# Two-attention decode kernel: the order of the first transfers, and the shape in which x is loaded

## Chip, core and metric

The kernel runs on one core of a Trainium2 chip. The metric is the device time of one execution in microseconds (us); lower is better.

## The reference

Two independent decode attentions, A and B, each for one query token. x has 576 elements; there are 32 query heads and 16 key/value heads of 128 elements, so that two query heads share a K and a V. The cache holds 8192 positions; A uses only the last 2048 of them, B uses all. Everything is bf16.

```python
W = min(4096, max(256, Sk // 4))                     # A: 2048
q = (x @ wq).reshape(B, Sq, Hq, Dh).transpose(0, 2, 1, 3)
k = jnp.repeat(k_cache[:, :, Sk - W:, :], rep, axis=1)   # B: all of k_cache
v = jnp.repeat(v_cache[:, :, Sk - W:, :], rep, axis=1)
scores = jnp.einsum("bhqd,bhkd->bhqk", q, k) * (Dh ** -0.5)
o = jnp.einsum("bhqk,bhkd->bhqd", softmax(scores), v)
return o.transpose(0, 2, 1, 3).reshape(B, Sq, Hq * Dh) @ wo
```

The output is A's row of 576 and B's row of 576, side by side. With wq and wo (576 x 4096 and 4096 x 576, 4.7 MB each) a call reads 102.76 MB.

## The kernel before

**Memory.** One SBUF tensor, `slots`, holds four areas of 4 MB: K slot 0, K slot 1 and a V area of two slots. Work goes in five groups (`NG`): group 0 is all of A, groups 1 to 4 are four key/value heads of B each. A group loads K slot 0 (4 MB), K slot 1 (4 MB) and V (8 MB). The wq tensors borrow the same areas before the first group: A's wq lies at the end of the V area, B's wq over K slot 1 and the beginning of V (`WQ`, L711). wo is loaded into areas that have come free at the end.

**Order.** Every operation is added with its engine and the resources that it reads and writes (`Program.add`). The waits are worked out from these; each engine then runs its own operations in the order in which they were added. All large transfers are issued by SP, on one queue, in this order before the change:

1. half of A's K slot 0 (`half_of_A(sp, 0, 0)`, L713): 128 rows of 16 KB. `emit` takes SP's first operation out of the list, whatever it is, and puts it ahead of the barrier at the program's start (L246 to L252);
2. A's wq, and 3. B's wq (`load`, L398): 128 rows of 36 KB each;
4. the other half of K slot 0 (`load_k(0, 0)`, L409), then K slot 1 for A as two halves (L411, L417), and V for A as four quarters (L429);
5. for B, per group, K slot 0, K slot 1 (L407) and V (L424); at the end wo in five pieces (L398).

Both halves of K slot 0 count on one semaphore (`k0`); PE begins to transpose K when it has reached 64, that is when both have landed. A's K slot 1 can be issued only when PE has read all of B's wq, which lies there.

**The query.** ACT issues two small loads of x, one for A and one for B (`load_x`, L366), each as 64 rows of nine elements into `xnine`. `twice` is a 64 x 128 selection matrix, copied by DVE from the identity (L437): one matmul (L440) multiplies `xnine` by it, so that row m of x comes out in partitions 2m and 2m + 1 of PSUM `misc`. `x_columns` (L449, four small DVE operations for each of A and B) puts the halves into the zero-padded `xpad`, with the help of the parity mask `par2`. `q_part` (L458) then makes q with 36 matmuls of 512 columns over wq, and `q_finish` turns it into columns (ACT L464, PE L469, DVE L473). On DVE the order is: `twice`, A's xpad, A's q columns, B's xpad, B's q columns, then twelve operations that build masks (L722 to L747), then copies out of the K transposes (L511).

**The stages of a group.** PE transposes K by 128 x 128 matmuls (L498), ACT and DVE copy the results (L508, L511), PE forms scores (L523), ACT takes the exponential (L549), PE transposes it (L561) and DVE masks it (L568), PE sums V (L590), DVE keeps the result (L608). In the last group the softmax weights of all groups are combined (L617 to L673) before the V sums. At the end PE multiplies by wo (L693), DVE and ACT copy out (L705) and SP stores (L707).

POOL fills constants at the start (`setup`, L375 to L377, and the selections of L383, which make the identity).

Of the kernel before, what the change touches and what calls it, by code (L numbers as in the profile page):

```python
# [4 lines left out]
BF16 = mybir.dt.bfloat16  # L5
# [9 lines left out]
SK = 8192  # L15
SCALE = DH ** -0.5
SLOT = 16384
UNIT = 4096
# [18 lines left out]
class Program:  # L37
# [15 lines left out]
    def add(self, eng, fn, reads=(), writes=(), dma=None, after=(), tag=None, inc=1, loop=None):  # L53
        op = Op(eng, fn, tuple(reads), tuple(writes), dma, tag, inc if dma is None or inc > 1 else 16, loop)
        deps = []
        for r in op.reads:
            w = self.writer.get(r)
            if w is not None:
                deps.append((w, True))
            if r[0] == "bank":  # L60
                deps += [(o, False) for o in self.readers.get(r, ())]
        for r in after:
            deps += [(o, False) for o in self.readers.get(r, ())]
        for r in op.writes:
            w = self.writer.get(r)
            if w is not None:
                deps.append((w, False))
            deps += [(o, False) for o in self.readers.get(r, ())]
        for r in op.reads:
            self.readers.setdefault(r, []).append(op)  # L70
        for r in op.writes:
            self.writer[r] = op
            self.readers[r] = []
        for o, raw in deps:
            if o is op:
                continue
            if o.dma is None and o.eng == eng and (not raw or eng in ("pe", "sp")):
                continue
            op.deps.append(o)
            o.needed = True  # L80
        op.order = len(self.ops)
        self.ops.append(op)
        return op
# [192 lines left out]
def bass_concat_heads__sliding_block_cached__gqa_block_cached__decode_kernel(  # L276
# [13 lines left out]
    xs = [A_x, B_x]  # L290
    ks = [A_k_cache, B_k_cache]
# [3 lines left out]
    W_A = min(4096, max(256, SK // 4))  # L295
# [12 lines left out]
    add = prog.add  # L308

    slots = nc.alloc_sbuf_tensor("slots", [128, 4 * SLOT], BF16)  # L310
# [3 lines left out]
    ident = nc.alloc_sbuf_tensor("ident", [128, 128], BF16)  # L314
    identf = nc.alloc_sbuf_tensor("identf", [128, 128], F32)
    pick = nc.alloc_sbuf_tensor("pick", [128, 4, 128], F32)
    pickB = nc.alloc_sbuf_tensor("pickB", [128, 4, 32], F32)
# [3 lines left out]
    selq = nc.alloc_sbuf_tensor("selq", [128, 4, 2], BF16)  # L321
    onesf = nc.alloc_sbuf_tensor("onesf", [128, 4], F32)
    qst = nc.alloc_sbuf_tensor("qst", [128, 1024], BF16)
    qcol = nc.alloc_sbuf_tensor("qcol", [128, 2, HQ], BF16)
    xnine = nc.alloc_sbuf_tensor("xnine", [64, 2, 9], BF16)
    twice = nc.alloc_sbuf_tensor("twice", [64, 128], BF16)
    xpad = nc.alloc_sbuf_tensor("xpad", [128, 2, 9, 32], BF16)
    par2 = nc.alloc_sbuf_tensor("par2", [128, 2], F32)
    maskV = nc.alloc_sbuf_tensor("maskV", [128, 4], F32)
# [11 lines left out]
    warm = nc.alloc_sbuf_tensor("warm", [128, 8], F32)  # L341
# [5 lines left out]
    misc = nc.alloc_psum_tensor("misc", [128, 512], F32)  # L347
# [4 lines left out]
    B_M = ("bank", 7)  # L352
# [4 lines left out]
    KS = [[("k", 0)], [("k", 1, 0), ("k", 1, 1)]]  # L357
    VS = [("v", 0), ("v", 1), ("v", 2)]
    koff = lambda s: s * SLOT
# [3 lines left out]
    def load_x(P):  # L363
        def go(act):
            with nc.allow_non_contiguous_dma(reason="small x load"):
                return act.dma_start(xnine[:, P, :], xs[P][0, 0, :].rearrange("(m r) -> m r", m=64))  # L366
        add("act", go, writes=[("xnine", P)], dma="x%d" % P)

    load_x(0)
# [1 line left out]


    def setup(pool):
        for t in (ident, xpad, selq, warm, identf, pick, pickB, qst):
            pool.memset(t[:], 0.0)  # L375
        pool.memset(onesf[:], 1.0)
        return pool.memset(opj[:], 0.0)  # L377

    add("pool", setup, writes=["ident", ("xpad", 0), ("xpad", 1), "selq", "ones", "warm", "identf", "pick", "pickB",
                               ("qst", 0), ("qst", 1), ("opj", 0), ("opj", 1)])  # L380

    def select(t, base_, pattern, mult):
# [18 lines left out]
    def load_k(g, s):  # L401
        dst = slots[:, koff(s):koff(s) + SLOT]

        def go(sp):
            if g:
                i = 4 * (g - 1) + s
                return sp.dma_start(dst, ks[1][0, i:i + 3:2, :, :].rearrange("e (p t) d -> p e (t d)", t=128))  # L407
            if s == 0:
                return half_of_A(sp, s, 1)  # L409
            op.also.append((32, half_of_A(sp, s, 0)))  # L410
            return half_of_A(sp, s, 1)  # L411
        op = add("sp", go, writes=KS[s], dma="k%d" % s, inc=64 if g or s else 32)

    def half_of_A(sp, s, m1):
        i = 8 * m1 + s
        src = ks[0][0, i:i + 7:2, SK - W_A:, :].rearrange("h (p t) d -> p h (t d)", t=64)
        return sp.dma_start(slots[:, koff(s) + m1 * 2 * UNIT:koff(s) + (m1 + 1) * 2 * UNIT], src)  # L417

    def load_v(g):
        dst = slots[:, VOFF:VOFF + 2 * SLOT]  # L420

        def go(sp):
            if g:
                return sp.dma_start(dst, vs[1][0, 4 * g - 4:4 * g, :, :].rearrange("h (p t) d -> p h (t d)", t=256))  # L424
            for i in range(4):
# [4 lines left out]
                if i < 3:  # L430
# [3 lines left out]

    add("dve", lambda dve: dve.tensor_copy(twice[:, :].rearrange("p (m e) -> p m e", e=2),  # L437
                                           bass.AP(tensor=ident, offset=0, ap=[[128, 64], [1, 64], [0, 2]])),
        reads=["ident"], writes=["twice"])
    add("pe", lambda pe: pe.matmul(misc[:, 320:338], lhsT=twice[:, :], rhs=xnine[:, :, :].rearrange("p a r -> p (a r)"),  # L440
                                   start=True, stop=True),
        reads=[("xnine", 0), ("xnine", 1), "twice"], writes=[B_M])

# [263 lines left out]
            reads=[("outsb", P, k) for k in range(P + 1)], writes=[("out", P)], dma="out%d" % P)  # L709

    WQ = [(4 * SLOT - WQ_W, [("v", 2)]), (SLOT, [("k", 1, 0), ("k", 1, 1), ("v", 0)])]  # L711

    add("sp", lambda sp: half_of_A(sp, 0, 0), writes=["first"], dma="k0", inc=32)  # L713
    for P in range(2):
        off, res = WQ[P]
        x_columns(P)
# [9 lines left out]
        reads=["kindA"], writes=["sameA"])  # L726
# [3 lines left out]
        reads=["sameB0"], writes=["sameB"])  # L730
# [3 lines left out]
    def pick_A(dve):  # L734
# [8 lines left out]
        reads=["sameB0", "pickB"], writes=["pickB"])  # L743
# [3 lines left out]
        reads=["four"], writes=["maskP"])  # L747
    for g in range(NG):
        for s in range(2):
            load_k(g, s)  # L750
        load_v(g)
        for s in range(2):
            q_stage(g, s)
        k_transpose(g, 0, 0)
        k_transpose(g, 1, 1)
        for u in range(2, 8):
            k_scores(g, u - 2, 2 * u)
            k_transpose(g, u, 2 * u + 1)
        k_scores(g, 6, 16)
        k_scores(g, 7, 17)  # L760
        softmax_exp(g)
        for c in range(2):
            softmax_transpose(g, c, 18 + c / 2)
        if g == NG - 1:
            weights_top(g)
            weights_exp(g)
            weights_sum(g)
            combine(range(NG - 1), (g, 19.3, LAST))
            o_columns(0)
        v_sums(g)  # L770
        v_keep(g)
# [47 lines left out]
```

## Time and profile before

| | us |
|---|---|
| three runs | 246.78, 246.80, 247.11; median 246.8 |
| the profiled execution, its own time | 246.78 |
| its span, first to last instruction | 245.3 |
| outside the span | 1.5 |
| A's x: issue to landing | 8.8 |
| B's x: issue to landing | 15.3 |
| A's wq: issue to landing | 17.2 |
| B's wq: issue to landing | 27.7 |
| spread of x (L440) starts | 17.32 |
| A's query (L458) starts | 18.67 |
| B's query (L458) starts | 29.55 |
| SP issues A's K slot 1 | 33.30 |
| first K transpose (L498) starts | 34.53 |

All times in views are microseconds from the start of the span. A line of a timeline has the start, the duration, the engine, the line of the kernel, the operation and its output and inputs; in brackets the engine's idle time before it and what ended it. SPq is SP's sequencer, PEld the weight load of TensorE. The trace has a record of each packet that a DMA engine moved as well, with start, duration and size; where a number comes from these and not from a view, the text says "packet records".

### The profile page before, as it was taken

The page shows a single profiled execution, that of the slowest core. Times are in us where ns is not written, and L with a number is a line of the kernel's source. Part 1 is how long each engine was busy: PE and PEld are TensorE (multiplying, and loading weights), DVE is VectorE, ACT ScalarE, POOL GpSimd, SP SyncE. Part 2 cuts the span into 40 slices and gives each one's busy share as a digit, 9 for nine tenths or more (in the row PEclk, how much of TensorE's full clock was granted, in tenths as well). Part 3 has the DMA queues.
Part 4 walks back from the last instruction along what each step waited for, and adds up shares of the span by engine and source line. Part 5 has one row for each costly group of instructions (what it writes and reads, how often), then busy time and mean ns, then how long its engine had stood idle before and what let it go on. Part 6 is the DMA issues. An engine that isn't in the chain of part 4 may idle for free. (4 is left out here: it accounts for less than half of the span.)

```text
span 245.3 us, 5212 instructions
## 1 busy us (share of the span) xinstructions
PE 161.8 (66%) x2325; PEld 115.8 (47%) x2325; DVE 87.8 (36%) x152; ACT 92.7 (38%) x96; POOL 6.3 (3%) x33
## 2 busy tenths in 40 slices
PE   0006188695368997184999454999647599845964
PEld 0002056563226684133878221978432687635753
DVE  0011039475206545202555312265522256533030
ACT  2000037575104776200778400577620378630000
POOL 5000000000000000000000000000000000000000
PEclk9999689998559999757899757599968799977699
DMA  7999989999999999999999999999999999999994
GB/s 313 444 451 397 423 345 417 430 427 430 446 425 427 450 470 417 395 438 433 492 402 481 406 395 427 427 460 460 395 406 427 438 470 438 438 397 439 416 406 176
DMA packets 4064, 102.88 MB, mean 419 GB/s; under 512 B 596, under 2 KB 728, under 8 KB 984
## 3 DMA queue, kind: packets, MB, share of 16 engines
q1 hardware_dynamic: 3896, 102.76, 97.7%
q8 instruction: 6, 0.10, 0.2%
q10 hardware_dynamic: 160, 0.00, 0.0%
q14 instruction: 2, 0.02, 0.0%
HBM read 102.76 MB, written 0.00 MB: 419 GB/s over the span
## 5 line engine op out<-in xcount | busy, mean ns | idle before, releaser
L508 ACT ACTIVATE kt<-ktps 128x1024 bf16<-128x1024 bf16 x80 | 79.3, 1039 | 84.1 <-PE ktps L498 84.0
L498 PE MATMUL ktps<-ident,slots 128*128 128x128 bf16 x1280 | 83.5, 227 | 16.3 <-PEq L214 15.7
L498 PEld LDWEIGHTS ktps<-ident,slots 128*128 128x128 bf16 x1280 | 77.3, 102 | 32.1 <-issue 32.0
L511 DVE COPY kt<-ktps 128x1024 bf16<-128x1024 bf16 x80 | 60.4, 772 | 48.9 <-PE ktps L498 48.9
L590 PE MATMUL opsum<-slots,ptm 128*32 128x512 bf16 x320 | 28.8, 536 | 14.3 <-PEq L214 14.3
L590 PEld LDWEIGHTS opsum<-slots,ptm 128*32 128x32 bf16 x320 | 14.0, 129 | 27.6 <-issue 25.6
L523 PE MATMUL sacc<-kt,qst 128*32 128x512 bf16 x320 | 25.4, 392 | 2.3 <-PEq L214 2.3
L608 DVE TENSOR_TENSOR vtmp<-opsum,maskV 128x512 f32<-128x512 f32 x4 | 2.8, 692 | 34.8 <-PE opsum L590 34.8
L561 PE MATMUL misc<-ident,psb 128*128 128x128 bf16 x40 | 4.6, 288 | 15.8 <-PEq L214 15.8
L549 ACT ACTIVATE psb<-sacc,stat 128x2048 bf16<-128x2048 f32 x5 | 9.8, 1967 | 9.7 <-DVE stat L538 9.7
L561 PEld LDWEIGHTS misc<-ident,psb 128*128 128x128 bf16 x40 | 3.5, 129 | 18.2 <-issue 18.2
L440 PE MATMUL misc<-xnine,twice 64*128 64x18 bf16 x1 | 0.2, 173 | 17.3 <-DMA xnine<-in_B_x_dram 17.3
L568 DVE TENSOR_TENSOR ptm<-misc,maskP 128x1024 bf16<-128x1024 bf16 x5 | 3.5, 692 | 16.0 <-PE misc L561 16.0
L523 PEld LDWEIGHTS sacc<-kt,qst 128*32 128x32 bf16 x320 | 5.0, 94 | 8.3 <-issue 4.7
L705 ACT ACTIVATE outsb<-ktps 64x144 bf16<-64x144 f32 x1 | 0.3, 287 | 21.5 <-PE ktps L693 21.5
L693 PE MATMUL ktps<-slots,opj 128*32 128x144 bf16 (+1 forms) x192 | 6.8, 247 | 2.3 <-DMA slots<-in_B_wo_dram 2.3
L440 PEld LDWEIGHTS misc<-xnine,twice 64*128 64x128 bf16 x1 | 0.1, 102 | 17.3 <-issue 17.3
L458 PE MATMUL turned<-slots,xpad 128*32 128x512 bf16 x36 | 3.7, 590 | 5.9 <-DMA slots<-in_B_wq_dram 5.9
L464 ACT ACTIVATE qrow<-opsum 128x512 bf16<-128x512 f32 x1 | 0.6, 597 | 18.4 <-PE opsum L458 18.4
L693 PEld LDWEIGHTS ktps<-slots,opj 128*32 128x32 bf16 x192 | 5.2, 97 | 3.8 <-DMA slots<-in_B_wo_dram 3.0
L473 DVE CAST qcol<-misc 128x32 bf16<-128x32 f32 x2 | 0.6, 300 | 15.4 <-PE misc L469 15.4
L449 DVE TENSOR_SCALAR xpad<-misc,par 128x5 bf16<-128x5 f32 (+1 forms) x8 | 1.2, 229 | 12.4 <-PE misc L440 12.4
(76 smaller groups left out, 58.2 us busy)
## 6 DMA issues: line engine op xcount, KB each, us to landing
slots<-in_B_k_cache_dram SPq DMA_DIRECT2D x8, 4096.0 KB
slots<-in_A_k_cache_dram SPq DMA_DIRECT2D x4, 2048.0 KB
slots<-in_A_v_cache_dram SPq DMA_DIRECT2D x4, 2048.0 KB
slots<-in_A_wq_dram SPq DMA_DIRECT2D x1, 4608.0 KB, 17.2
slots<-in_B_wq_dram SPq DMA_DIRECT2D x1, 4608.0 KB, 27.7
slots<-in_A_wo_dram SPq DMA_DIRECT2D x1, 4608.0 KB, 19.7
slots<-in_B_wo_dram SPq DMA_DIRECT2D x1, 3024.0 KB, 26.5
slots<-in_B_wo_dram SPq DMA_DIRECT2D x1, 1008.0 KB, 9.3
```

The lines of the kernel that those rows point to most:

```text
L449: add("dve", lambda dve, dst=dst, o=320 + 9 * P + i, n=n, e=e: dve.tensor_scalar(dst, misc[:, o:o + n], par2[:, e:e + 1], None, ALU.mult), ...
L458: ins = pe.matmul((turned if P else opsum)[32 * j:32 * j + 32, :], lhsT=xpad[:, P, u, :], rhs=slots[:, o:o + 512], start=(u == 0), stop=(u ...
L498: ins = pe.matmul(ktps_bf[q][:, t * 128:(t + 1) * 128], lhsT=slots[:, o:o + 128], rhs=ident[:, :], start=True, stop=True, is_transpose=True)
L508: add("act", lambda act, src=src, dst=dst: act.activation(dst, src, ACT.Copy), reads=[("bank", q)], writes=[("kt", u % NKT, q)], tag="e%d% ...
L511: add("dve", lambda dve, src=src, dst=dst: dve.tensor_copy(dst, src), reads=[("bank", q)], writes=[("kt", u % NKT, q)], tag="e%d%d" % (u, q))
L523: ins = pe.matmul(sacc[32 * j:32 * j + 32, :], lhsT=qst[:, o:o + 32], rhs=rhs, start=(u == 0 and e == 0), stop=True, skip_group_check=True)
L549: return act.activation(dst, src, ACT.Exp, bias=st(C_NB + g), scale=SCALE, accum_out=st(C_L + g))
L561: ins = pe.matmul(dst[:, t * 128:(t + 1) * 128], lhsT=psb[:, o:o + 128], rhs=ident[:, :], start=True, stop=True, is_transpose=True)
L568: return dve.tensor_tensor(ptm[:, c * 1024:(c + 1) * 1024].rearrange("p (t y) -> p t y", t=8), dst.rearrange("p (t y) -> p t y", t=8), mas ...
L590: ins = pe.matmul(opsum[64 * j + 32 * x:64 * j + 32 * x + 32, :], lhsT=ptm[:, o:o + 32], rhs=v[:, at[0], at[1], :, :, b:b + 128], start=(n ...
L608: add("dve", lambda dve: dve.tensor_tensor(vtmp[:, :, :], src, by, ALU.mult), reads=[B_O, w], writes=["vtmp"], tag="keep")
L693: ins = pe.matmul(ktps[P + j // 2][32 * j:32 * j + 32, 0:w], lhsT=opj[:, P, at:at + 32], rhs=slots[:, o:o + w], start=(jj == 0), stop=(jj ...
```

## The change

x comes as 16 rows of 36 elements for A and for B. `twice` becomes four selection matrices of 16 x 128, one for each quarter of such a row; POOL clears it (it is no longer written as a whole) and one DVE copy sets its ones. Four matmuls, one for each quarter, accumulate into the same place of PSUM as the single one did. The half of K slot 0 is no longer loaded ahead of everything: SP's first operation, which is issued ahead of the barrier, is now A's wq, and both halves of K slot 0 follow B's wq. Everything else is as it was.

```diff
-    xnine = nc.alloc_sbuf_tensor("xnine", [64, 2, 9], BF16)
-    twice = nc.alloc_sbuf_tensor("twice", [64, 128], BF16)
+    xnine = nc.alloc_sbuf_tensor("xnine", [16, 2, 36], BF16)
+    twice = nc.alloc_sbuf_tensor("twice", [16, 4, 128], BF16)
...
-                return act.dma_start(xnine[:, P, :], xs[P][0, 0, :].rearrange("(m r) -> m r", m=64))
+                return act.dma_start(xnine[:, P, :], xs[P][0, 0, :].rearrange("(m r) -> m r", m=16))
...
-        for t in (ident, xpad, selq, warm, identf, pick, pickB, qst):
+        for t in (ident, twice, xpad, selq, warm, identf, pick, pickB, qst):
             pool.memset(t[:], 0.0)
...
-            if s == 0:
-                return half_of_A(sp, s, 1)
-            op.also.append((32, half_of_A(sp, s, 0)))
-            return half_of_A(sp, s, 1)
-        op = add("sp", go, writes=KS[s], dma="k%d" % s, inc=64 if g or s else 32)
-
-    def half_of_A(sp, s, m1):
-        i = 8 * m1 + s
-        src = ks[0][0, i:i + 7:2, SK - W_A:, :].rearrange("h (p t) d -> p h (t d)", t=64)
-        return sp.dma_start(slots[:, koff(s) + m1 * 2 * UNIT:koff(s) + (m1 + 1) * 2 * UNIT], src)
+            for m1 in range(2):
+                i = 8 * m1 + s
+                src = ks[0][0, i:i + 7:2, SK - W_A:, :].rearrange("h (p t) d -> p h (t d)", t=64)
+                ins = sp.dma_start(dst[:, m1 * 2 * UNIT:(m1 + 1) * 2 * UNIT], src)
+                if m1 == 0:
+                    op.also.append((32, ins))
+            return ins
+        op = add("sp", go, writes=KS[s], dma="k%d" % s, inc=64)
...
-    add("dve", lambda dve: dve.tensor_copy(twice[:, :].rearrange("p (m e) -> p m e", e=2),
-                                           bass.AP(tensor=ident, offset=0, ap=[[128, 64], [1, 64], [0, 2]])),
-        reads=["ident"], writes=["twice"])
-    add("pe", lambda pe: pe.matmul(misc[:, 320:338], lhsT=twice[:, :], rhs=xnine[:, :, :].rearrange("p a r -> p (a r)"),
-                                   start=True, stop=True),
-        reads=[("xnine", 0), ("xnine", 1), "twice"], writes=[B_M])
+    add("dve", lambda dve: dve.tensor_copy(bass.AP(tensor=twice, offset=0, ap=[[512, 16], [130, 4], [8, 16], [1, 2]]),
+                                           bass.AP(tensor=ident, offset=0, ap=[[128, 16], [0, 4], [1, 16], [0, 2]])),
+        reads=["ident", "twice0"], writes=["twice"])
+
+    def x_spread(pe):
+        for c in range(4):
+            ins = pe.matmul(misc[:, 320:338], lhsT=twice[:, c, :], rhs=xnine[:, :, 9 * c:9 * c + 9],
+                            start=(c == 0), stop=(c == 3))
+        return ins
+    add("pe", x_spread, reads=[("xnine", 0), ("xnine", 1), "twice"], writes=[B_M])
...
-    add("sp", lambda sp: half_of_A(sp, 0, 0), writes=["first"], dma="k0", inc=32)
```

More of the change, by code (lines that the diff above doesn't have):

```diff
@@ L377, in setup @@
         return pool.memset(opj[:], 0.0)
-    add("pool", setup, writes=["ident", ("xpad", 0), ("xpad", 1), "selq", "ones", "warm", "identf", "pick", "pickB",
+    add("pool", setup, writes=["ident", "twice0", ("xpad", 0), ("xpad", 1), "selq", "ones", "warm", "identf", "pick", "pickB",
                                ("qst", 0), ("qst", 1), ("opj", 0), ("opj", 1)])
```

## Prediction

> **What bounds the kernel now.** I read the page from the top: engines, slices, queues.
>
> ```profile
> PE 161.8 (66%) x2325; PEld 115.8 (47%) x2325; DVE 87.8 (36%) x152; ACT 92.7 (38%) x96; POOL 6.3 (3%) x33
> ...
> DMA  7999989999999999999999999999999999999994
> ...
> q1 hardware_dynamic: 3896, 102.76, 97.7%
> ```
>
> No compute engine is over two thirds busy. The transfers that SP issues (q1) fill 97.7% of 16 engines' span, 239.7 of 245.3 us. So the kernel is one stream of 102.76 MB, and only a stretch in which the DMA engines stand still can be won. There is one slice below 9 in the middle, the sixth from the left (slice 5, 0-based), besides the first and the last. The table of windows of 1 us shows that place (columns: stretch and its length, busy us of each engine, clock, DMA share, GB/s):
>
> ```profile
> 32.00:33.00 1.00, 1.00 (x16) 0.32 (x8) 0.00 (x0) 0.00 (x0) 0.00 (x0) 0.61 0.99 426
> 33.00:34.00 1.00, 0.29 (x10) 0.04 (x2) 0.00 (x0) 0.60 (x1) 0.00 (x0) 1.00 0.39 164
> 34.00:35.00 1.00, 0.68 (x13) 0.62 (x14) 0.71 (x4) 0.00 (x0) 0.00 (x0) 1.00 0.65 197
> 35.00:36.00 1.00, 1.00 (x22) 1.00 (x20) 0.97 (x7) 0.82 (x1) 0.00 (x0) 1.00 0.77 328
> ```
>
> The stream falls from 426 to 164 GB/s and is back after 36. SP's own waits and the timeline there name the cause:
>
> ```profile
> SPq L417 <- PE turned L458: 30.3, 1, 30.3
> ```
>
> ```profile
> 32.51 0.74 PE L458 MATMUL turned<-slots,xpad 128*32 128x512 bf16 x8
> 33.30 1.20 SPq L417 DMA_DIRECT2D slots<-in_A_k_cache_dram  x2
> ```
>
> SP waits until the last B-query matmul has read B's wq, since A's second K slot lies over it; it issues that K load at 33.30. The packet records show the last packets of the transfer ahead (the second half of A's first K slot) ending engine by engine from 33.38 to 34.03, and the first packets of the new load starting from 34.64 to 35.10: 1.34 us from issue to first packet. Summed over the 16 engines, the idle time between 33.0 and 35.5 is **1.11 us** of the stream. Nowhere else between 6 and 240 us do the records show one.
>
> The chain of waits shows that this counts at the end:
>
> ```profile
> 227.62 5.08 PE opsum L590 x57
> ...
> 232.72 0.33 SPq L398
> ...
> 233.09 10.06 DMA slots<-in_B_wo_dram
> 243.15 0.04 issue
> ```
>
> The last wo loads are issued at 232.72, but the wo transfer ahead of them keeps the engines until 237.26 and later. With 1.34 us to the first packet they come 3.2 us early, and the stream, not PE, sets 243.15. What is taken out of the stream comes off the end.
>
> [...] once started, one x packet goes with each wq packet (7.0, 8.4, 9.8 us, steps of 1.37), but the first x packet goes at 5.58, 4.2 us after its issue at 1.39, when an engine has passed about seven 16 KB packets. [...]
>
> **The change part by part.**
>
> 1. *Order of the stream.* Before: half of K slot 0, A's wq, B's wq, the other half. After: A's wq, B's wq, both halves. The bytes ahead of K slot 1 are the same, so K slot 0 still ends at 33.4 to 34.0. What moves is wq. The records price the half slot at 8 packets of 0.611 us per engine, 4.9 us, and a wq at 8 of 1.364 us, 10.9 us. So A's wq lands about 12.6 to 13.4 (18.6 before) and B's at 23.6 to 24.3 (29.2 before). The B query starts on landing and takes, as now, 3.75 us from its first matmul (29.55) to SP's issue (33.30). K slot 1 is issued near **28.3**, when over 5 us of K slot 0 are still to be moved. The 1.34 us to the first packet are hidden, and the gap goes.
>    Worth: 1.11 us of idle engines. The restart too: 12 of the 16 first packets after the gap took 0.87 instead of 0.611 us, 12/16 x 0.26 = 0.19. Sum **1.30 us**. The start keeps its slow first packets; with 36 KB packets they may cost nothing to 0.2 us more. I take off 0.1.
> 2. *The hoisted issue.* SP's instruction ahead of the barrier is now wq's (0.38 us) in place of half a K slot (0.69). First packet at 1.41 us in either case. Behind the barrier SP issues B's wq and two halves, 0.53 + 2 x 0.6, done near 3.2. Cost nothing; the cover is the 10.9 us of the first wq.
> 3. *x.* Eight x rows per engine become two, with two semaphore writes as before: 4 x packets per engine in place of 10. Each costs the stream about 0.012 us, so 0.07 us are won. Arrival: not before 1.39 + 1.34 = 2.7 plus four turns; at the latest, if seven packets of 36 KB pass first, 1.66 + 7 x 1.364 = 11.2, then three more turns of 1.37, 15.3. I take 15. The spread may then be later than A's wq, but 2 us earlier than the 17.3 of now.
> 4. *Four matmuls.* Three more at up to 0.17 us (the one of now takes 0.173), at most 0.5 us. On the path x to spread to xpad to A query to xpad B to B query: 0.8 us for spread and xpad, 5.7 from the first A-query matmul to B's xpad ready (18.67 to 24.41), 0.5 for the new matmuls. From x at 15.3: 22.3, before B's wq at 23.6. Hidden by wq's landing. If that cover went, it would cost at most 0.5.
> 5. *POOL and DVE.* One memset of 512 elements more: near 0.53 us (pick, 128x512). It holds up ident, behind which par2 and twice wait on DVE (at 4.6 now, then 5.2). The copy into twice has 128 elements a row as before, 0.26. All under x, which comes no earlier than about 7. Nothing.
> 6. *Later.* K slot 1 lands 1.3 us earlier, and so does every transfer behind it. Who could be late next is an issue whose release does not move: V at 75.3 with the queue full to 83.5, V at 112.0 with 122.3, wo at 212.7 with 219.2, the last wo at 232.7 with 237.3. The smallest margin is the last, 4.5 less 1.34. The first K transposes follow a pause of PE of 5 us where there was almost none, [...] DVE's twelve mask operations (34.4 to 36.7, ahead of the first K copies now) move to about 30. PE now stands idle from 44.7 to 47.0 waiting for K slot 1, so this has room.
>
> Sum against the profiled execution's own time: 246.78 - 1.30 + 0.1 - 0.07 = 245.5; since a restart elsewhere or the landing of the slowest engine may eat a little, I take **1.2 us: 245.6**. That execution lies at the lower end of the three runs, 0.02 under their median of 246.8.
>
> **The rivals.**
>
> *x comes too late (slower).* x now stands behind 36 KB packets from the start. From the spread to SP's K issue the path takes 0.8 + 0.5 + 5.7 + 3.75 = 10.8 us. The issue must be made by about 32.0 (33.4 - 1.34), so the spread by 21.2; at 22.5 the gap is as large as now, and beyond that each us costs one. If the first x packet had to wait for both wq transfers (16 packets, 23.5 us) and the other turns fall among K packets, the spread comes at 25.4, the K issue at 36.2, the first packet at 37.5: a gap of 3.8 + 0.2 in place of 1.3, **249.5**. For it: the 4.2 us that x waits now are not explained by turns. Against: the wait now is seven packets, not sixteen, and the four turns after it end at 15.3.
>
> *The gain is given back (same).* Earlier landings meet a PE that is not earlier, because its clock falls in other places, and the last wo issue comes late. This needs PE's last V sums to be over 3.2 us later against the stream[...]. Time **246.7**. V sums of the first stage already start 3.7 us after V has landed (69.6 against 65.9), for a reason the views do not give.
>
> *Half the gain.* The engines finish K slot 0 more unevenly, or the start on 36 KB packets is slower: 0.6 us, **246.2**.
>
> *The change does not do what it says:* wq would not be first on the wire. The hoist takes whatever SP operation stands first, and with the half slot gone that is wq; I give it nothing.
>
> **How the numbers follow.** Gap closed, 245.6 (245.3 to 245.9): 0.78. Half the gain, 246.2: 0.08. Given back: 0.08. x too late: 0.06. What a measurement can tell from no change is about 0.2%, 0.5 us. Faster by more: 0.78 + 0.08 = 0.86; same 0.08; slower 0.06. The range of 245.2 to 246.3 takes in the first two cases.
>
> **What would show it.** SP's wait for the B query ends near 28.3 instead of 33.3; the windows from 33 to 36 stay above 380 GB/s; A's query starts between 13 and 17; PE resumes on K slot 1 near 45.7 instead of 46.97; the last landing is at 241.9 instead of 243.15. A gap elsewhere, a spread after 21 us, or a wo issue that comes after its queue has run dry would prove me wrong.

## The result, and the profile after

The changed kernel takes **245.37 us** (median of 6 runs, 245.18 to 245.63), the kernel before 246.99 (6 runs): a ratio of 0.9937 with a 95% interval of 0.9924 to 0.9950, or 1.6 us less. A second measurement, 245.46 beside 247.35, gave 0.9925 (0.9912 to 0.9938). The profiled execution took 245.18 us, its span is 243.8 us; before these were 246.78 and 245.3.

The page of the changed kernel, slices and queues:

```profile
DMA  9999999999999999899999999999989999989994
...
q1 hardware_dynamic: 3896, 102.76, 98.3%
q10 hardware_dynamic: 64, 0.00, 0.0%
```

The 8 in the sixth slice has become a 9, and the same bytes fill more of a shorter span. The x queue has 64 packets in place of 160. SP's waits and its timeline around the change (start, duration, instruction):

```profile
SPq L411 <- PE turned L460: 26.3, 1, 26.3
```

```profile
28.86 1.20 SPq L411 DMA_DIRECT2D slots<-in_A_k_cache_dram  x2
30.10 1.25 SPq L427 DMA_DIRECT2D slots<-in_A_v_cache_dram  x2
```

SP still waits for B's query before K slot 1, but the wait ends at 28.86 instead of 33.30, and the windows of 1 us show what this does to the stream (the last columns are clock, DMA share and GB/s; a packet counts whole in the window in which it starts, so a share can pass 1):

```profile
32.00:33.00 1.00, 0.00 (x0) 0.00 (x0) 0.22 (x1) 0.00 (x0) 0.00 (x0) 0.89 1.07 459
33.00:34.00 1.00, 0.00 (x0) 0.00 (x0) 0.00 (x0) 0.00 (x0) 0.00 (x0) 0.50 1.08 459
34.00:35.00 1.00, 0.33 (x4) 0.36 (x5) 0.00 (x0) 0.00 (x0) 0.00 (x0) 0.50 0.88 377
35.00:36.00 1.00, 1.00 (x12) 1.00 (x10) 0.00 (x0) 0.28 (x1) 0.00 (x0) 0.50 1.11 475
```

Before, the last three had 164, 197 and 328 GB/s. The chain of waits ends as before, with wo:

```profile
227.83 4.97 PE opsum L592 x59
...
232.82 0.33 SPq L398
...
233.19 8.42 DMA slots<-in_B_wo_dram
241.61 0.04 issue
```

PE's last V sums end at the same time as before (232.80 against 232.70). The last wo landing, which waits for the stream, comes 1.54 us earlier (241.61 against 243.15). That is the gain of the span.

The packet records tell when it arises. I add up the bytes moved on q1 since the span's start (a packet under way in proportion) and divide by 0.4287 MB/us, the full rate (102.76 MB over 239.7 us of packet time on 16 engines). The unit is thus one us of full-rate stream:

| us of full-rate stream moved by | 4 us | 13 us | 33 us | 60 us |
|---|---|---|---|---|
| before | 2.14 | 10.98 | 31.10 | 56.61 |
| changed | 2.09 | 11.16 | 31.34 | 58.17 |
| lead | -0.05 | 0.18 | 0.24 | 1.56 |

Between 33 and 60 us the lead grows by **1.32 us**: the gap and the slow restart. The other 0.2 comes earlier, but is no larger than the scatter: the profiled execution of the second measurement leads by 0.07 at 33 us, and between 33 and 60 us it wins 1.34 more.

### The profile page after: what moved, and what is told of

The parts are those of the page before. It is cut to its first block, busy times and chain, and to the rows that moved or that the text cites. A ratio compares the mean times of both kernels' runs of the same rounds, so it can differ in the third digit from the quotient of the medians.

```text
span 243.8 us, 5219 instructions
## 1 busy us (share of the span) xinstructions
PE 164.0 (67%) x2328; PEld 119.3 (49%) x2328; DVE 88.2 (36%) x152; ACT 93.2 (38%) x96; POOL 6.8 (3%) x34
## 3 DMA queue, kind: packets, MB, share of 16 engines
q1 hardware_dynamic: 3896, 102.76, 98.3%
HBM read 102.76 MB, written 0.00 MB: 422 GB/s over the span
## 5 line engine op out<-in xcount | busy, mean ns | idle before, releaser
L500 PE MATMUL ktps<-ident,slots 128*128 128x128 bf16 x1280 | 86.0, 231 | 19.9 <-PEq L214 17.4
L500 PEld LDWEIGHTS ktps<-ident,slots 128*128 128x128 bf16 x1280 | 79.8, 104 | 35.5 <-issue 35.4
L592 PE MATMUL opsum<-slots,ptm 128*32 128x512 bf16 x320 | 27.0, 510 | 13.4 <-PEq L214 13.4
L525 PE MATMUL sacc<-kt,qst 128*32 128x512 bf16 x320 | 25.4, 392 | 2.3 <-PEq L214 2.3
L592 PEld LDWEIGHTS opsum<-slots,ptm 128*32 128x32 bf16 x320 | 13.5, 124 | 25.5 <-issue 22.6
L485 POOL COPY qst<-qcol 128x32 bf16<-128x32 bf16 x8 | 1.7, 211 | 152.2 <-PE sacc L525 152.2
L460 PE MATMUL opsum<-slots,xpad 128*32 128x512 bf16 x36 | 4.0, 630 | 2.6 <-DMA slots<-in_A_wq_dram 2.6
## 6 DMA issues: line engine op xcount, KB each, us to landing
slots<-in_B_wo_dram SPq DMA_DIRECT2D x1, 3024.0 KB, 25.5
```

What stands on the lines that cost most here:

```text
L460: ins = pe.matmul((turned if P else opsum)[32 * j:32 * j + 32, :], lhsT=xpad[:, P, u, :], rhs=slots[:, o:o + 512], start=(u == 0), stop=(u ...
L500: ins = pe.matmul(ktps_bf[q][:, t * 128:(t + 1) * 128], lhsT=slots[:, o:o + 128], rhs=ident[:, :], start=True, stop=True, is_transpose=True)
L525: ins = pe.matmul(sacc[32 * j:32 * j + 32, :], lhsT=qst[:, o:o + 32], rhs=rhs, start=(u == 0 and e == 0), stop=True, skip_group_check=True)
L592: ins = pe.matmul(opsum[64 * j + 32 * x:64 * j + 32 * x + 32, :], lhsT=ptm[:, o:o + 32], rhs=v[:, at[0], at[1], :, :, b:b + 128], start=(n ...
```

## The experiments

Three theories were put to the chip. *Theory 1*: the gain is the closed gap, with something for an earlier start of the stream; the shape of x is worth nothing. *Theory 2*: 16 rows are needed, or have a part in it. *Theory 3*, in two forms: all of it is the gap, or, the other way round, having A's wq first is what is good.

**The order alone, x as before.** The changed kernel with 64 rows and one matmul.

```diff
-    return act.dma_start(xnine[:, P, :], xs[P][0, 0, :].rearrange("(m r) -> m r", m=16))
+    return act.dma_start(xnine[:, P, :], xs[P][0, 0, :].rearrange("(m r) -> m r", m=64))
...
```

> Only the order of the transfers is changed (A's wq hoisted, both halves of K slot 0 behind B's wq); x stays at 64 rows and one matmul. Theory 1 (the gain is the closed gap ahead of K slot 1 and an earlier start of the stream; the shape of x is worth nothing): the ten turns of x end near 18 us (first x packet near 4.7, as in the changed kernel, then nine turns of 1.37), the spread comes at about 18, before the 21.2 at which the gap would open; SP issues K slot 1 at 29 to 29.5, no gap, 245.4 us, 1.6 under the kernel before. Theory 2 (16 rows are needed, since 64 rows come too late behind 36 KB packets): the spread comes after 21.2, at 23 to 25, the gap is there again, 246.5 to 249 us.

Measured: 245.48 us, ratio 0.9932 (0.9920 to 0.9944), as much as the whole change. Its timeline:

```profile
17.76 0.17 PE L438 MATMUL misc<-xnine,twice 64*128 64x18 bf16 x1 [17.76 <-DMA xnine<-in_B_x_dram]
18.74 4.03 PE L456 MATMUL opsum<-slots,xpad 128*32 128x512 bf16 x36 [0.81 <-DVE xpad L447]
...
24.62 2.13 PE L456 MATMUL turned<-slots,xpad 128*32 128x512 bf16 x36 [0.91 <-DMA slots<-in_B_wq_dram]
26.79 1.20 SPq L411 DMA_DIRECT2D slots<-in_A_k_cache_dram  x2
```

x comes at 17.76 and delays A's query by five us, but B's query still starts with B's wq, and K slot 1 is issued at 26.79, earlier than the 29 that I had expected. (B's query took only 2.13 us for its 36 matmuls, where it took 3.70 in the kernel before and 4.03 in the changed one. It began 1.85 us after A's had ended, and the trace records full clock all through it, from 23.14 to 29.97.) Theory 2 falls in its first form.

**x alone.** The kernel before with 16 rows and four matmuls; half of K slot 0 stays first.

> Only x is changed (16 rows, four matmuls); half of K slot 0 stays the first transfer. Theory 1: x lands near 9 instead of 17 us, but A's query still waits for A's wq at 18.6; SP issues K slot 1 at 33.3 as before, the gap of 1.1 us stays, 246.9 us, 0 to 0.1 under the kernel before. Theory 2 (x has a part in the gain): 246.5 us or less.

Measured: 247.09 us beside 247.19, ratio 0.9993 (0.9984 to 1.0001). x is spread at 8.74 instead of 17.32, SP's wait for B's query is as long as before, and the gap is 1.22 us in the packet records:

```profile
8.74 0.25 PE L443 MATMUL misc<-xnine,twice 16*128 16x18 bf16 x4 [8.74 <-DMA xnine<-in_B_x_dram]
```

```profile
SPq L417 <- PE turned L462: 30.3, 1, 30.3
```

Theory 2 falls altogether: an earlier x only waits for A's wq (`xpad` is written at 9.65, and A's query starts at 18.53, released by the landing of A's wq).

**One half of K slot 0 between the two wq.** A's wq is first, but only one half lies behind B's wq.

```diff
     for P in range(2):
         x_columns(P)
+        if P:
+            add("sp", lambda sp: half_of_A(sp, 0, 0), writes=["first"], dma="k0", inc=32)
         load(... wqs[P] ...)
...
```

> The changed kernel with one half of K slot 0 moved between A's and B's wq, so that only one half (4.9 us) lies between B's wq and K slot 1, as in the kernel before, while A's wq is still the hoisted first transfer. Theory 1: the first packet comes at 1.05 us as in the changed kernel, the gap of 1.1 us and the slow restart (0.2) are back: 246.6 us, 0.4 under the kernel before and 1.2 to 1.3 over the changed one. Theory 3 (all of the gain is the gap, the earlier start is only a shift of the profile's zero): 247.0 us. If having wq first is what is good, whatever lies behind it: 245.4 us.

Measured: 247.13 us, ratio 1.0000 (0.9992 to 1.0008). Having wq first brings no time while the gap is there. Theory 1 as I had put it gave 0.4 us to the earlier start and was wrong in that number. The test is not a clean one, though: the profiled execution (247.99 us, the slowest of 14, so its sizes are not typical) has the first packet at 1.03 us and yet a longer gap, behind which a small gain of the start could hide:

```profile
30.22 4.03 PE L462 MATMUL turned<-slots,xpad 128*32 128x512 bf16 x36 [11.14 <-DMA slots<-in_B_wq_dram]
34.29 1.20 SPq L417 DMA_DIRECT2D slots<-in_A_k_cache_dram  x2
```

B's wq had landed on its first engine 1.48 us before its last (0.65 before), the query waits for the last one, and the windows show PE at half clock (0.50) up to 34 us. The gap is 2.3 us there.

**No cover at all.** Both halves of K slot 0 ahead of B's wq: nothing is queued behind it.

```diff
+        if P:
+            add("sp", lambda sp: half_of_A(sp, 0, 0), writes=["first"], dma="k0", inc=32)
+            load_k(0, 0)
         load(... wqs[P] ...)
...
```

> The changed kernel with both halves of K slot 0 ahead of B's wq: nothing is queued between B's wq and K slot 1. Theory 1: B's wq lands near 34, its query takes 4.05 us, the issue 1.34 to the first packet: the stream stands still for 5.4 to 5.8 us ahead of K slot 1, restart 0.2, all of it on the end: 250.9 to 251.4 us. Rival (later stages take up a part, the end is not the stream's): under 249.5 us.

Measured: 252.26 us beside 247.19, ratio 1.0209 (1.0196 to 1.0223); 251.83 in the profiled execution. Windows of 1 us:

```profile
33.00:34.00 1.00, 0.00 (x0) 0.00 (x0) 0.00 (x0) 0.00 (x0) 0.00 (x0) 0.50 0.01 0
34.00:35.00 1.00, 0.71 (x8) 0.30 (x12) 0.00 (x0) 0.00 (x0) 0.00 (x0) 0.50 0.00 0
...
38.00:39.00 1.00, 0.33 (x4) 0.00 (x0) 0.00 (x0) 0.60 (x1) 0.00 (x0) 0.62 0.00 0
39.00:40.00 1.00, 0.92 (x16) 0.86 (x17) 0.65 (x4) 0.02 (x1) 0.00 (x0) 1.00 0.98 246
```

In six windows in a row (0 GB/s from 33 to 39) no packet of the stream starts. The idle time is 6.3 us by the packet records, and the execution is 6.65 us longer than the changed kernel's (251.83 against 245.18): all of it reaches the end, and the slow restart with it. The rival, that later stages take up a part, falls. I had expected a gap of up to 5.8 and at most 251.4 us: I had left out the time from the last packet of wq to the first matmul (0.4 us in the kernel before and in the changed one) and the spread of the engines.

**x made late.** The order of the changed kernel, 64 rows, and one load of 64 rows more ahead of the two.

```diff
+    add("act", load_spare, writes=["xspare"], dma="spare")   # 64 rows of x, read by nothing
     load_x(0)
     load_x(1)
```

> The order of the changed kernel with x at 64 rows, and one more load of 64 rows of x (into a tile that nothing reads) issued by ACT ahead of the two: five turns more on each DMA engine. Theory 1 with the prediction's path: first x packet at 4.7, 14 turns of 1.37 behind it, spread near 24, then 0.85 + 5.7 + 4.05 us to SP's issue of K slot 1 near 35 and 1.34 to the first packet: a gap near 2.6 us ahead of K slot 1 and 0.2 for the restart, 248.0 to 248.3 us. Rival (the query is not on the path to that issue, or x packets do not take turns with 36 KB packets one by one): 245.4 to 246.0 us, no gap.

Measured: 249.12 us beside 247.30, ratio 1.0065 (1.0047 to 1.0083). The timeline of the profiled execution (249.53 us):

```profile
25.17 0.17 PE L443 MATMUL misc<-xnine,twice 64*128 64x18 bf16 x1 [25.17 <-DMA xnine<-in_B_x_dram]
...
32.05 3.81 PE L461 MATMUL turned<-slots,xpad 128*32 128x512 bf16 x36 [0.91 <-DVE xpad L452]
35.91 0.55 SPq L416 DMA_DIRECT2D slots<-in_A_k_cache_dram  x1
```

B's query now waits for xpad and not for wq, and SP's issue follows the spread by 10.74 us. The gap is 3.3 us. The spread came 1.2 us later than I had expected and the time lies 0.8 over my range; apart from the gap, the stream had moved 0.6 us less by 33 us than in the order alone (30.66 against 31.24), which I cannot account for. The path of the prediction's slower rival was thus taken here, with the spread at 25.17; it isn't with 16 rows (spread at 11.01) or 64 (17.76).

**A plain first transfer.** The kernel before, whose first transfer is a block of the same bytes and rows, read from one place. Half of the data in A's first K slot is thus not A's.

```diff
-    add("sp", lambda sp: half_of_A(sp, 0, 0), writes=["first"], dma="k0", inc=32)
+    add("sp", lambda sp: sp.dma_start(slots[:, 0:2 * UNIT], ks[1][0, 0, :, :].rearrange("(p t) d -> p (t d)", t=64)),
+        writes=["first"], dma="k0", inc=32)
```

> The kernel before, with its first transfer replaced by one of the same bytes and the same 16 KB rows whose source is one contiguous block (128 rows of B's first head) instead of four heads' rows in turn; the scores of half of A's first slot are thus formed from other data. Theory 1a (the source pattern sets how long SP takes to issue and when the first packet comes): SP's first issue takes 0.4 instead of 0.69 us, the first packet comes at 1.05 instead of 1.41, 246.6 us, 0.35 to 0.4 under the kernel before, gap as before. Theory 1b (the earlier first packet comes with the larger rows or the larger transfer of wq): issue and first packet as before, 247.0 us.

Measured: 247.31 us beside 247.30, ratio 1.0006 (0.9997 to 1.0015). Half of theory 1a holds: SP's issue takes 0.46 us instead of 0.69 and the first packet comes at 1.02 instead of 1.41, so between these two runs it is the source pattern that delays it. But the time does not follow. The first 16 packets took 0.99 to 1.83 us where they took 0.73 to 1.01 before, and at 33 us the stream had moved 31.09 us of data, against 31.10. An earlier first packet was paid back within the first packets.

**The gap filled with V, order and x as before.** One quarter of A's V goes ahead of K slot 1.

```diff
+    def load_v_quarter():
+        src = vs[0][0, 12:16, SK - W_A:, :].rearrange("h (p t) d -> p h (t d)", t=64)
+        add("sp", lambda sp: sp.dma_start(slots[:, VOFF + 6 * UNIT:VOFF + 8 * UNIT], src),
+            writes=[("v", 2)], dma="vq")
...
             load_k(g, s)
+            if g == 0 and s == 0:
+                load_v_quarter()
```

> The kernel before with its order and its x (half of K slot 0 first, 64 rows), but with one quarter of A's V, whose place is free once A's query has read A's wq, issued ahead of K slot 1 instead of behind it: 4.9 us more are queued between B's wq and K slot 1. Theory 1 (the gap ahead of K slot 1 is all there is to win): SP issues K slot 1 at 33.3 as before, but the stream goes on with the V quarter to about 39, no gap, 1.3 to 1.6 us under the kernel before, as much as the changed kernel. K slot 1 lands 3.6 us later than before, so PE waits longer in the first group and V for group 1 is issued near 79 instead of 75, still ahead of the 82 at which its queue would run dry. Theory 3 (A's wq has to be first): no more than 0.3 us under the kernel before.

The changed kernel ran beside it:

> The changed kernel once more, beside the fill with V on one chip: 0.6 to 0.7% under the kernel before by either theory. Under theory 1 the two are within 0.2% of each other; under theory 3 this one is 1 us faster than the fill with V.

Measured: 245.88 us for the fill, ratio 0.9944 (0.9928 to 0.9960), and 245.46 for the changed kernel, ratio 0.9925 (0.9912 to 0.9938), beside 247.35 before. SP issues K slot 1 at 33.09, as late as ever, but the stream runs on with the V quarter:

```profile
33.00:34.00 1.00, 0.29 (x8) 0.17 (x4) 0.00 (x0) 0.60 (x1) 0.00 (x0) 1.00 1.15 492
34.00:35.00 1.00, 0.55 (x11) 0.58 (x11) 0.93 (x4) 0.00 (x0) 0.00 (x0) 1.00 0.73 311
35.00:36.00 1.00, 1.00 (x22) 1.00 (x19) 0.96 (x9) 0.90 (x1) 0.00 (x0) 1.00 1.15 492
```

Closing the gap in this way, without wq first and without the new x, brings 1.4 us. Theory 3 in its form "wq must be first" falls; the gap is nearly all there was to win.

Between the fill and the changed kernel lie 0.4 us; run by run they hardly overlap (245.46 to 246.61 against 245.23 to 245.56). The profiled execution of the fill (246.48 us) shows a second narrow place. K slot 1 stands behind 4.9 us more of transfers there, PE starts A's V sums at 74.51 instead of 69.64, and the issue of V for group 1, which waits for them, comes later as well:

```profile
81.00 0.55 SPq L424 DMA_DIRECT2D slots<-in_B_v_cache_dram  x1
```

I had expected it near 79. The first engine runs dry at 82.22, and the first packet of V comes at 82.34, again 1.34 us after its issue. The engines hardly stand still, but 14 of the first 16 packets of 64 KB take 2.5 to 3.4 us instead of 2.42, and the stream loses 0.6 us between 82 and 86 by the packet records. That would cover the 0.4 us; whether it is as large in the runs that were not profiled is not shown.

## Why the prediction was right, step by step

The forecast was 245.6 (245.2 to 246.3) and faster; measured 245.37 beside 246.99.

1. *Order of the stream: right.* The issue of K slot 1 was put at 28.3 and came at 28.86. The last packet of B's wq ended at 24.37 instead of at most 24.3, and B's query took 4.03 us instead of 3.7, as A's did. Before, the clock records had 0.50 from 25.96 to 32.78 and 1.00 for the last stretch of the query. (Here the trace's first clock record, of full clock, begins at 29.37, when the query was over; the windows show 1.00 where there is no record yet. That the query had half clock throughout is thus my estimate from its time, the 4.03 us that it took at a recorded 0.50 with one half between the wq.) Neither mattered with 5 us of K slot 0 still queued. The gain of this step, 1.11 + 0.19 = 1.30 us, was measured at 1.32 in the packet records, and two other ways of changing the gap (no cover, V fill) move the time by about its length.
2. *The hoisted issue: wrong in its fact, right in its price.* "First packet at 1.41 us in either case" fails: with wq's plain pattern it comes at 1.03, and the barrier ends at 0.80 instead of 1.39. But the first 16 wq packets took 1.4 to 2.4 us instead of 1.364, and at 4 us the stream was 0.05 behind the kernel before. After the plain first transfer nothing was left of the earlier packet at 33 us. With wq first a little may be: the five profiled executions of that order, without the one with the late x, had then moved 31.17 to 31.34 us of stream, the four with half of K slot 0 first 30.99 to 31.16. That is no more than two executions of the changed kernel differ by, and no run shows it in the time. Why the first packets are slower when they come earlier is open.
3. *x: cost right, arrival wrong.* I put the spread at 15, counting seven packets ahead of the first x packet as in the kernel before. The changed kernel has it here:

```profile
11.01 0.25 PE L441 MATMUL misc<-xnine,twice 16*128 16x18 bf16 x4 [11.01 <-DMA xnine<-in_B_x_dram]
...
13.89 4.03 PE L460 MATMUL opsum<-slots,xpad 128*32 128x512 bf16 x36 [2.64 <-DMA slots<-in_A_wq_dram]
```

   The first x packet came 3.9 us after its issue, nearly as in the kernel before (4.2), though the packets ahead were over twice as large; in all ten traces it took 3.8 to 4.3. So this wait looks like one of time rather than of a number of packets; what it consists of stays open. The turns after it, 1.37 us each, are as predicted: one packet of x to each row of wq (4.72, 6.09, 7.46 and 8.83 us, counted from the earliest). So is their number: before, the x queue had 128 packets of 18 bytes and 32 of 4, ten for each of 16 engines, and now it has 32 of 72 bytes and 32 of 4, four for each. Those of 4 bytes end a load: its semaphore was counted up 16 times, each 0.28 to 0.41 us after the end of one of them.
4. *Four matmuls: right.* 0.25 us for all four, hidden behind wq.
5. *POOL and DVE: right.* The memset costs what was forecast (from the barrier to the identity 3.65 us instead of 3.19), but the earlier barrier makes up for it: the identity is ready at 4.45 instead of 4.58.
6. *Later stages: right.* The windows above show half clock (0.50) at the first K transposes, which follow a pause of PE of 4.90 us; by the clock records it lasted from 32.78 to 39.61, for 4.9 us of the transposes. The issue of group 1's K slot 0 moved by 1.5 us, from 44.21 to 45.69, 17 us before the first engine would have run dry. PE went on to K slot 1 at 46.16 (45.7 predicted) without waiting for it.

*The sum* was too small by 0.4 us. I took 0.2 off the 1.30 as a precaution against slower first packets and uneven landings, and those cost nothing net. Between 33 and 60 us the profiled executions with the changed order (the changed kernel twice, and the order alone) each moved 26.8 us of stream; the three with the order of before (the kernel before, x alone, the plain first transfer) moved 25.5, 25.2 and 25.3, with gaps of 1.1 to 1.3 us. Gap and restart were thus worth 1.3 to 1.6 us, and the kernel before, from which I had taken the 1.30, is the lowest of these. What the gap was in the runs that were not profiled cannot be seen. That the forecast of the time is off by only 0.2 is luck in part: I started from 246.78, and the median of all runs of the kernel before is 246.99.

*The rivals.* The slower one was right in its path (10.8 us predicted from the spread to SP's issue, 10.74 measured with x made late). With the spread at 25.17 the gap was 3.3, which puts its opening at 21.9 instead of 21.2, and the 249.5 that it gave for a spread at 25.4 was nearly met (249.12). The spread came at 11.0, and with 64 rows at 17.8: there were at least 4 us left, so it deserved less than its chance. "Given back" did not come: PE's last V sums did not move, and the stream still had work queued at 232.8. "Half the gain" did not come either: the engines ended K slot 0 within 0.6 us of each other, as before, and the start lost nothing.

## What to carry to other kernels

In a kernel that is one long stream, look for the one issue that waits for a consumer, and compare the time from the landing of what is consumed to the first packet of the new load (here 0.4 + 3.7 + 1.34 us, and the engines' unevenness on top) with the work queued behind that landing (4.9 us before, 9.8 after). If the queue is shorter, reorder what is queued until it isn't: here K served (1.6 us less), and so did V (1.4 us less). Then look at the issues that come later because of it: the V fill opened a second narrow place near 82 us. What makes an operand arrive earlier is worth nothing as long as it still waits for another one: here x, spread at 8.74 instead of 17.32, left the time at 247.09 beside 247.19.

## What the runs showed of the hardware

- After the stream had stood still, its first packets were slower: for 16 KB 0.85 to 0.92 us in 12 of 16 after the gap of the kernel before, and up to 1.2 us after the other gaps, instead of 0.611. With 64 KB it was 2.5 to 3.4 us in 14 of 16 instead of 2.42, though the engines had stood still for only 0.1 us on average (the V fill). At the start, packets of 36 KB took 1.4 to 2.6 us (1.40 to 2.44 in the changed kernel) instead of 1.364.
- A load whose source goes through four heads in turn took SP 0.69 us to issue at the start, a plain one of the same bytes 0.46, and the first packet came at 1.41 us with the one and at 1.02 with the other.
- A small load on a busy set of engines waited about 4 us for its first packet (4.2 in the kernel before, 3.9 in the changed one, 3.8 to 4.3 in ten traces), with 16 KB and with 36 KB packets ahead of it.
- The same 36 matmuls of a query took 4.03 us with the clock at 0.50 throughout (30.22 to 34.25, one half between the wq) and 2.13 us with the clock at 1.00 throughout (24.62 to 26.75, the order alone).
